# Two layers of decode attention on one core: gate and up by column halves, copies shared by two engines, filler transposes, and another map of the buffer between the layers

## The chip, the core and the metric

The kernel runs on one core of a Trainium2 chip. The metric is the device time of one execution in microseconds (us); the median of several runs counts, and less is better. The core has a matrix engine, TensorE (PE in the profile, with PEld for its weight loads), and three engines for other work: VectorE (DVE), ScalarE (ACT) and GpSimd (POOL). SyncE (SP) issues the large transfers (DMAs) from the chip's memory into the core's buffer, SBUF. TensorE writes its results to PSUM, from which VectorE and ScalarE read.

## The reference

One token for each of two sequences goes through two rounds of attention over a long cache and a gated feed-forward block. Both rounds use the same weights and the same cache. Sizes: 512 features, 32 query heads of 128, 8 key/value heads, 32768 cached positions, 1792 hidden features, all float32.

```python
def _A_ref(x, k_cache, v_cache, wq, wo):          # x: (2, 1, 512)
    q = (x @ wq).reshape(B, 1, 32, 128)            # 32 query heads, 4 to a K/V head
    k, v = repeat(k_cache, 4), repeat(v_cache, 4)  # (2, 8, 32768, 128) each
    p = softmax((q . k) * 128 ** -0.5)
    return (p . v).reshape(B, 1, 4096) @ wo

def _B_ref(x, w_gate, w_up, w_down):
    return (gelu(x @ w_gate) * (x @ w_up)) @ w_down

for _ in range(2):
    x = x + _A_ref(layernorm(x), k_cache, v_cache, wq, wo)
    x = x + _B_ref(layernorm(x), w_gate, w_up, w_down)
```

## The kernel before

**Tiling and buffer.** A (K/V head, sequence) combination is called a pair; a layer has 16 pairs, and layer 1 takes them in the reverse order. All weights, K and V go through one SBUF tile, `mem`, of 104 units. A unit is 512 float32 columns on 128 partitions, 256 KB. K of a pair has 64 units (16 MB), V as well. They come in pieces of 32 units, but for the last two pairs of layer 0 (`K_SPLIT`, `V_SPLIT`), which come in pieces down to 4 units.

**What sets the order of the transfers.** `add` puts every transfer of the program in one list, `stream`, in the order in which it will be needed. `take` finds a place in `mem` for the transfer at the head of the list, `give` returns the place of a piece that has been used, and `pump` issues transfers from the head as long as places are found (L157, the only line that issues loads from SP). For the pieces around the change of layers, `plan` names the place in units: a table written by hand. So a DMA stands in SP's queue until the instructions that read the previous holder of its place are done, and SP issues in order: a DMA that waits holds all DMAs behind it.

**Between the layers.** The last pair of layer 0 is the first of layer 1. Its V (64 units, 0 to 64) and the last `KEEPK` pieces of its K (8 units each) stay in `mem` and aren't loaded again. The remaining units serve, one after the other, `wo` (the output projection's weights), four transfers of gate and up weights (`gu`, 7 units each), four of the down weights (`wd`), four of the query weights of layer 1 (`wq`, 8 units each), and then the remaining K of that pair. The plan of before:

```python
out["gu", 0, i] = [80, 87, 94, 80][i]
out["wd", 0, i] = [88, 92, 96, 100][i]
out["wq", 1, i] = [80, 88, 96, 80][i]
put(K_SPLIT, "k", 1, last, [88, 96, 80, 64, 72, 88])
```

gu 0 and gu 1 have places that are free before the layer's end; gu 2 covers the place of `wo`, and gu 3 that of gu 0.

**A pair.** `scores` (L316) multiplies the queries with the K pieces into the PSUM tile `S`; `softmax` takes the maximum (L320), the exponential (L336) and transposes the probabilities through the PSUM tile `T` (L339, L340); `values` (L358) multiplies them with the V pieces into the PSUM tile `A`; `combine` scales `A` to the SBUF tile `big` (L365, VectorE, 512 columns) and gathers the heads by four products with a selection matrix (L369) into `oT` (L370); after every second pair `project` (L375) multiplies with `wo` into the PSUM tile `W`.

**Between attention and feed-forward.** `residual` copies `W` to SBUF on ScalarE and sums it (L389), and adds the residual and the mean with products on TensorE (L380, L382, L392) into `xin` (L393); `complete`, called later, does the same a second time for the residual stream. `spread` works out the layer norm's scale, with a power on GpSimd (L261). `feedforward` multiplies gate and up by rows of the weights (L419: a transfer holds 128 of the 512 input features, all 1792 columns of both matrices), applies gelu (L428 to L434), transposes (L439, L440) and multiplies with the down weights (L446). `queries` (L283) does the query projection, and scales and transposes the result (L292, L295, L298). `finish` (L406 to L411) writes the output.

## Time and profile before

| | before |
|---|---|
| time, median of 3 runs | 2595.84 us (2595.5 to 2597.18) |
| the profiled execution | 2596.09 us |
| its span | 2594.1 us, so 1.99 us lie around it |
| TensorE busy | 1373.1 us, 53% of the span |
| bytes moved | 1109.86 MB, mean 428 GB/s |
| L316 waiting for K | 549.0 us |
| L358 waiting for V | 497.6 us |

The span runs from the first to the last thing the profiler saw of the kernel. In a row of a timeline stand the start in us, the length, the engine, the line, the operation, what it writes and reads, how many instructions are put together, and in brackets how long the engine was idle before and what ended the wait. In a row of windows stand the stretch, its length, the busy time and number of instructions of PE, PEld, DVE, ACT and POOL, and then three numbers: the granted clock of TensorE as a share of full speed, the busy share of the DMA engines, and GB/s. "SPq" rows are DMAs at the moment of their issue.

### The profile page before, as it was taken

How to read it: one execution, taken by the hardware profiler on the slowest of the kernel's cores; microseconds unless marked ns; L12 is line 12 of the kernel's file. 1: busy time of each engine (PE TensorE's matmuls, PEld its weight loads, DVE VectorE, ACT ScalarE, POOL GpSimd, SP SyncE). 2: the span in 40 equal slices, each digit the busy share in tenths (PEclk: the TensorE clock that was granted, in tenths of full speed). 3: DMA queues.
4: the chain of work that ended last, by engine and by line, in shares of the span. 5: the costliest groups of instructions: out<-in, count | busy, mean ns of one | idle time of the engine just before them, and what ended most of it. 6: DMA issues, size and time to landing. Idle time of an engine off the chain costs nothing.

```text
span 2594.1 us, 20074 instructions
## 1 busy us (share of the span) xinstructions
PE 1373.1 (53%) x9434; PEld 399.3 (15%) x9434; DVE 152.5 (6%) x399; ACT 52.0 (2%) x140; POOL 2.9 (0%) x9
## 2 busy tenths in 40 slices
PE   3654555454445445455577454555555554554556
PEld 1111111111111111111122111111111111111112
DVE  0000000000000000000001000000000000000000
ACT  0000000000000000000000000000000000000000
POOL 0000000000000000000000000000000000000000
PEclk7677767777777777777778777767767767777677
DMA  9999999999999999999999999999999999999997
GB/s 423 431 428 434 432 434 431 432 435 436 429 432 429 435 435 433 429 428 429 409 384 438 433 433 430 433 433 432 433 432 434 432 435 432 430 434 430 436 432 334
DMA packets 28306, 1109.86 MB, mean 428 GB/s; under 512 B 3392, under 2 KB 3520, under 8 KB 3776
## 3 DMA queue, kind: packets, MB, share of 16 engines
q1 hardware_dynamic: 27936, 1108.36, 99.2%
q8 instruction: 74, 1.21, 0.2%
q10 hardware_dynamic: 288, 0.22, 0.0%
q14 instruction: 8, 0.07, 0.0%
HBM read 1108.56 MB, written 0.00 MB: 427 GB/s over the span
## 4 chain that ended last, share of the span: by engine, by line
DMA 59%; PE 27%; another core or an unknown queue 12%; DVE 1%; issue 0%; ACT 0%; SPq 0%; DVEq 0%; ACTq 0%
DMA mem<-in_vt 49%; PE A L358 16%; DMA mem<-in_kt 10%; PE S L316 7%; PE W L375 1%; PE small L369 1%; PE S L419 1%; PE W L446 0%; DVE big L365 0%; PE small L382 0%; DMA mem<-in_wq 0%; PE T L339 0%; DMA mem<-in_gu 0%; PE small L283 0%
## 5 line engine op out<-in xcount | busy, mean ns | idle before, releaser
L316 PE MATMUL S<-mem,qpad 128*32 128x512 f32 x4096 | 590.0, 739 | 550.2 <-DMA mem<-in_kt 549.0
L358 PE MATMUL A<-mem,pT 128*16 128x512 f32 x4096 | 580.8, 729 | 497.7 <-DMA mem<-in_vt 497.6
L316 PEld LDWEIGHTS S<-mem,qpad 128*32 128x32 f32 x4096 | 150.7, 132 | 980.3 <-issue 707.9
L358 PEld LDWEIGHTS A<-mem,pT 128*16 128x16 f32 x4096 | 128.4, 112 | 921.2 <-issue 740.3
L320 DVE TENSOR_REDUCE mx<-S 128x1 f32<-128x512 f32 x64 | 44.3, 692 | 1137.9 <-PE S L316 1137.9
L336 ACT ACTIVATE big<-S,bias 128x512 f32<-128x512 f32 x64 | 43.4, 683 | 2411.5 <-DVE bias L332 2411.5
L339 PE MATMUL T<-cst,big 128*128 128x128 f32 x256 | 54.9, 352 | 68.4 <-ACT big L336 40.4
L365 DVE TENSOR_SCALAR big<-A,linv 128x512 f32<-128x512 f32 x32 | 24.0, 751 | 1056.5 <-PE A L358 1056.5
L369 PE MATMUL small<-cst,big 128*128 128x4 f32 x256 | 36.2, 265 | 29.8 <-DVE big L365 29.8
L340 DVE COPY pT<-T 128x512 f32<-128x512 f32 x64 | 44.3, 692 | 91.6 <-PE T L339 91.6
L339 PEld LDWEIGHTS T<-cst,big 128*128 128x128 f32 x256 | 35.5, 175 | 83.3 <-ACT big L336 67.1
L369 PEld LDWEIGHTS small<-cst,big 128*128 128x128 f32 x256 | 33.4, 204 | 61.4 <-DVE big L365 61.4
L329 PE MATMUL small<-cst,nm 128*128 128x128 f32 x32 | 10.3, 322 | 34.2 <-DVE nm L327 34.2
L283 PE MATMUL small<-mem,xpad 128*32 128x512 f32 x128 | 21.0, 786 | 11.8 <-DMA mem<-in_wq 11.1
L375 PE MATMUL W<-mem,oT 128*2 128x512 f32 x128 | 25.0, 864 | 4.1 <-DVE oT L370 4.1
L419 PE MATMUL S<-mem,xpad 128*32 128x256 f32 x224 | 19.6, 471 | 3.6 <-DMA mem<-in_gu 3.1
L342 PEld LDWEIGHTS small<-ls,cst 128*128 128x128 f32 x64 | 14.4, 276 | 0.0
L329 PEld LDWEIGHTS small<-cst,nm 128*128 128x128 f32 x32 | 4.2, 133 | 64.9 <-DVE nm L327 62.8
L336 ACT ACTIVATION_READ_ACCUMULATOR big<-S,bias 128x1 f32 x64 | 12.6, 196 | 0.0
L446 PE MATMUL W<-mem,pT 128*2 128x512 f32 x56 | 11.3, 913 | 1.0 <-DVE pT L440 1.0
L342 PE MATMUL small<-ls,cst 128*128 128x2 f32 x64 | 11.8, 254 | 0.0
L419 PEld LDWEIGHTS S<-mem,xpad 128*32 128x32 f32 x224 | 9.0, 131 | 11.7 <-issue 4.2
(61 smaller groups left out, 100.2 us busy)
## 6 DMA issues: line engine op xcount, KB each, us to landing
mem<-in_kt SPq DMA_DIRECT2D x24, 2048.0 KB, 38.1
mem<-in_wq SPq DMA_DIRECT2D x8, 2048.0 KB, 10.6
mem<-in_wo SPq DMA_DIRECT2D x16, 1024.0 KB, 51.3
mem<-in_gu SPq DMA_DIRECT2D x8, 1792.0 KB, 39.3
mem<-in_vt SPq DMA_DIRECT2D x3, 4096.0 KB, 43.6
mem<-in_kt SPq DMA_DIRECT2D x2, 6144.0 KB, 37.9
mem<-in_vt SPq DMA_DIRECT2D x3, 2048.0 KB, 48.1
mem<-in_vt SPq DMA_DIRECT2D x6, 1024.0 KB, 51.4
```

The costliest lines, as they stand in the source:

```text
L283: nc.tensor.matmul(qp[32 * t:32 * t + 32, :], window(k, v), w[:, 4 * v + t, :], start=(k == 0 and v == 0), stop=(k == KC - 1 and v == 1))
L316: nc.tensor.matmul(S[32 * t:32 * t + 32, u, :], qpad[:, at_q - 4 * c:at_q + 32 - 4 * c], w[:, QUAD * i + t, :], start=(same_u[0] == 8 * u ...
L320: nc.vector.tensor_reduce(mx[:, u:u + 1], S[:, u, :], axis=AX.X, op=OP.max)
L336: nc.scalar.activation(p[u], S[:, u, :], AF.Exp, bias=bias, scale=SCALE, accum_out=ls[:, u:u + 1])
L339: nc.tensor.transpose(T[:, u, k * P:(k + 1) * P], p[u][:, k * P:(k + 1) * P], ident)
L340: nc.vector.tensor_copy(pT[:, u].rearrange("p k r -> p (k r)"), T[:, u, :])
L342: nc.tensor.matmul(m[:, :2], same, ls, start=True, stop=True)
L358: nc.tensor.matmul(A[32 * t:32 * t + 16, :], pT[:, u, k, 32 * t + 16 * e:32 * t + 16 * e + 16], w[:, QUAD * i + t, :], start=(j == 0), sto ...
L365: nc.vector.tensor_scalar(md, A, linv, None, op0=OP.mult)
L369: nc.tensor.matmul(m[:, :REP], md[:, c * P:(c + 1) * P], head[:, c, :], start=(c == 0), stop=(c == 3))
L375: nc.tensor.matmul(W[32 * t:32 * t + NB, :], oT[:, t, :], w[:, t, :], start=first, stop=final)
L419: nc.tensor.matmul(S[32 * t:32 * t + 32, which, :FN], window(k, v), w[:, FR * which + r, :], start=(k == 0 and v == 0), stop=(k == KC - 1 ...
```

## The change

There are five parts.

1. **The plan.** `KEEPK` is 3, so 24 units of K (64 to 88) stay between the layers, and one K piece of 2 MB fewer is loaded. All other transfers between the layers use the two places 88 to 96 and 96 to 104 in turn, until the kept pieces have been used. The table follows in the diff.
2. **Gate and up by column halves.** The weights are stored anew (`halves`): transfers 0 and 1 hold the first 1024 columns of both matrices (8 units each), 2 and 3 the other 768 (6 units each). The first half accumulates in `S`, the second in `T`, and gelu runs on each half by itself; the down products of the first half come before the transposes of the second.
3. **Shared copies.** `wide` splits a copy of 512 columns from PSUM into a half on ScalarE and a half on VectorE. `combine`, `residual`, `queries` and `finish` use it.
4. **Transposes in place of selection products.** `combine` and `residual` transpose the copy and sum the parts on VectorE; `complete` and its second gather are gone, its addition is one VectorE instruction. The matrix of averages is a broadcast of one column.
5. **Filler transposes.** `warm(n)` puts n transposes of the identity on TensorE, into a PSUM bank that nobody reads then: in the last pair of each layer ahead of every later V piece and in `combine`, further in `residual` and `finish`, after each gate/up transfer, and before the third down transfer.

In the stream, `wo` now stands ahead of a pair's second V piece instead of its last.

```diff
-KEEPK = 2
+KEEPK = 3
...
-    put(K_SPLIT, "k", 0, last, [32, 40, 48, 56, 80, 88, 64, 72])
+    put(K_SPLIT, "k", 0, last, [32, 40, 48, 56, 88, 64, 72, 80])
...
-        out["gu", 0, i] = [80, 87, 94, 80][i]
-        out["wd", 0, i] = [88, 92, 96, 100][i]
-        out["wq", 1, i] = [80, 88, 96, 80][i]
-    put(K_SPLIT, "k", 1, last, [88, 96, 80, 64, 72, 88])
+        out["gu", 0, i] = [88, 96, 88, 96][i]
+        out["wd", 0, i] = [88, 92, 96, 102][i]
+        out["wq", 1, i] = [88, 96, 88, 96][i]
+    put(K_SPLIT, "k", 1, last, [88, 96, 64, 72, 80])
...
+    def wide(dst, src, scale=None, totals=None):
+        h = 256
+        kw = [{}, {}] if totals is None else [{"accum_out": totals[:, i:i + 1]} for i in range(2)]
+        nc.scalar.activation(dst[:, h:], src[:, h:], AF.Copy, scale=1.0 if scale is None else scale, **kw[1])
+        if totals is None:
+            nc.vector.tensor_scalar(dst[:, :h], src[:, :h], 1.0 if scale is None else scale, None, op0=OP.mult)
+        else:
+            nc.vector.tensor_scalar(dst[:, :h], src[:, :h], 1.0, 0.0, op0=OP.mult, op1=OP.add, **kw[0])
+
+    def warm(n, bank=T[:, 0]):
+        for i in range(n):
+            nc.tensor.transpose(bank[:, :P], ident, ident)
...
+        for s, m in parts:
+            if s and n == len(ORDER) - 1:
+                warm(6)
...
-    def combine(linv, oT, b):
+    def combine(linv, oT, b, busy):
         md = big()
-        nc.vector.tensor_scalar(md, A, linv, None, op0=OP.mult)
-
+        wide(md, A, scale=linv)
+        warm(busy)
         m = small()
         for c in range(4):
-            nc.tensor.matmul(m[:, :REP], md[:, c * P:(c + 1) * P], head[:, c, :], start=(c == 0), stop=(c == 3))
-        nc.vector.tensor_copy(oT[:, :, b], m[:, :REP])
+            nc.tensor.transpose(m[:, c * P:(c + 1) * P], md[:, c * P:(c + 1) * P], ident)
+        warm(busy)
+        mt = m[:, :]
+        diag = bass.AP(tensor=mt.tensor, offset=mt.offset, ap=[mt.ap[0], [1, REP], [P + REP, 4], [32, 4]])
+        nc.vector.tensor_reduce(oT[:, :, b], diag, axis=AX.XY, op=OP.add)
...
+    def gathered(totals=None):
+        ws = big()
+        wide(ws, W, totals=totals)
+        warm(3)
+        m = small()
+        for c in range(KC):
+            nc.tensor.transpose(m[:, c * P:(c + 1) * P], ws[:, c * P:(c + 1) * P], ident)
+        ys = wk.tile([P, KC, NB], F32, name="ys")
+        src = m.rearrange("p (c t r) -> p c r t", c=KC, t=4)[:, :, :NB, :]
+        nc.vector.tensor_reduce(ys, src, axis=AX.X, op=OP.add)
+        return ys
...
+        def gelu(e):
+            gt, ut = both[e][:, 0, :FN], both[e][:, 1, :FN]
+            w = big()
+            a, th = w[:, :FN], w[:, FN:]
+            pr = hT[:, 4 + nj * e:4 + nj * e + nj, :].rearrange("p j r -> p (j r)")
+            nc.scalar.activation(a, gt, AF.Square, scale=cube)
+            nc.vector.tensor_scalar(pr, gt, hrr, None, op0=OP.mult)
+            nc.vector.scalar_tensor_tensor(a, a, 1.0, gt, op0=OP.add, op1=OP.mult)
+            nc.scalar.activation(th, a, AF.Tanh, scale=root)
+            nc.vector.tensor_tensor(pr, pr, ut, op=OP.mult)
+            nc.vector.scalar_tensor_tensor(th, th, 1.0, pr, op0=OP.add, op1=OP.mult)
+            return th
...
+            warm(6, A)
+            if i % 2 == 1:
+                th.append(gelu(e))
+        hidden(0, th[0])
+        down(0)
+        hidden(1, th[1])
+        down(1)
+        warm(4, A)
+        down(2)
+        down(3)
```

Where the instructions stand is shown for three places. The names are those of the tiles; "x4" counts equal instructions in a row. First the order in which SP issues the transfers around the change of layers, from the last pair's V on; before:

```order
L157 DMA mem<-in_vt 128x16384
L157 DMA mem<-in_vt 128x8192
L157 DMA mem<-in_vt 128x4096
L157 DMA mem<-in_vt 128x2048
L157 DMA mem<-in_wo 128x2048
L157 DMA mem<-in_vt 128x2048
L157 DMA mem<-in_gu 128x3584 x4
L157 DMA mem<-in_wd 128x2048 x3
L157 DMA mem<-in_wd 128x1024
L157 DMA mem<-in_wq 128x4096 x4
L157 DMA mem<-in_kt 128x4096 x11
```

and in the changed kernel:

```order
L152 DMA mem<-in_vt 128x16384
L152 DMA mem<-in_wo 128x2048
L152 DMA mem<-in_vt 128x8192
L152 DMA mem<-in_vt 128x4096
L152 DMA mem<-in_vt 128x2048 x2
L152 DMA mem<-in_gu 128x4096 x2
L152 DMA mem<-in_gu 128x3072 x2
L152 DMA mem<-in_wd 128x2048 x3
L152 DMA mem<-in_wd 128x1024
L152 DMA mem<-in_wq 128x4096 x4
L152 DMA mem<-in_kt 128x4096 x10
```

`wo` moved ahead of the later V pieces, the gate/up transfers are 8, 8, 6 and 6 units in place of four of 7, and one piece of K is gone.

Second, TensorE from the end of layer 0's last V piece to the first gate/up products; before:

```order
L358 MATMUL A<-mem,pT 16x512 x64
L369 MATMUL small<-cst,big 128x4 x4
L375 MATMUL W<-mem,oT 2x512 x4
L380 MATMUL small<-xpad,cst 128x8
L382 MATMUL small<-cst,big 128x2 x4
L392 MATMUL small<-cst,total 128x8
L419 MATMUL S<-mem,xpad 32x256 x14
L256 MATMUL small<-sq,avg 128x8
L419 MATMUL S<-mem,xpad 32x256 x42
```

and in the changed kernel, where L369 is `values`, L255 a filler, L380 the transposes of `combine`, L390 `project`, L400 to L413 `residual` and L466 gate/up:

```order
L255 MATMUL T<-cst 128x128 x6
L369 MATMUL A<-mem,pT 16x512 x4
L255 MATMUL T<-cst 128x128 x2
L380 MATMUL small<-cst,big 128x128 x4
L255 MATMUL T<-cst 128x128 x2
L390 MATMUL W<-mem,oT 2x512 x4
L255 MATMUL T<-cst 128x128 x3
L400 MATMUL small<-cst,big 128x128 x4
L411 MATMUL small<-xpad,cst 128x8
L413 MATMUL small<-cst,totals 128x8 x2
L255 MATMUL T<-cst 128x128 x2
L466 MATMUL S<-mem,xpad 32x256 x16
```

The selection products (L369 and L382 of before) are transposes, two products take the place of one for the total, and fillers stand between the steps.

Third, VectorE from the last pair's `combine` on, with the engines for which an instruction waits; before (L365 is the copy of 512 columns in `combine`, L393 writes `xin`, L429 to L434 are gelu):

```order
L365 TENSOR_SCALAR big<-A,linv 128x512 [waits DVE_49,PE_49,Activation_49]
L370 COPY oT<-small 128x4 [waits PE_49]
L393 COPY xpad<-small 128x4x2 [waits PE_49]
L254 TENSOR_TENSOR sq<-xpad 128x8 [waits DVE_49]
L258 ISA sq,var<-small,cst 128x8 [waits PE_49]
L258 ISA var 128x1
L263 SCALAR_TENSOR_TENSOR hrr<-rstd 128x1 [waits Pool_49]
L399 COPY xn<-small 128x8 [waits PE_49]
L429 TENSOR_SCALAR big<-big 128x256 [waits Activation_49]
L430 SCALAR_TENSOR_TENSOR big<-S,rstd,big 128x256 [waits DVE_49]
L433 SCALAR_TENSOR_TENSOR big<-big,S 128x256 [waits Activation_49]
L434 SCALAR_TENSOR_TENSOR big<-big,hrr,S 128x256 [waits DVE_49]
```

and in the changed kernel (L248 and L250 are VectorE's halves of a shared copy, L437 to L441 gelu of one half):

```order
L248 TENSOR_SCALAR big<-A,linv 128x256 [waits Activation_49]
L385 TENSOR_REDUCE oT<-small 128x4 [waits PE_49]
L250 TENSOR_SCALAR big,totals<-W 128x256 [waits Activation_49]
L403 TENSOR_REDUCE ys<-small 128x8 [waits PE_49]
L415 TENSOR_TENSOR xpad<-small,ys 128x4x2 [waits DVE_49,PE_49]
L417 TENSOR_TENSOR xn<-ys,xT 128x8
L266 TENSOR_TENSOR sq<-xpad 128x8 [waits DVE_49]
L270 ISA sq,var<-small,cst 128x8 [waits PE_49]
L270 ISA var 128x1
L474 SCALAR_TENSOR_TENSOR hrr<-rstd 128x1 [waits Pool_49]
L475 TENSOR_SCALAR cube<-rstd 128x1
L476 TENSOR_SCALAR root<-rstd 128x1
```

VectorE's half of a copy waits for ScalarE, which holds the other half of the same PSUM tile. Further on in the same order:

```order
L437 TENSOR_SCALAR pT<-S,hrr 128x256 [waits Activation_49]
L438 SCALAR_TENSOR_TENSOR big<-big,S 128x256
L440 TENSOR_TENSOR pT<-pT,S 128x256 [waits DVE_49]
L441 SCALAR_TENSOR_TENSOR big<-big,pT 128x256 [waits DVE_49,Activation_49]
L437 TENSOR_SCALAR pT<-T,hrr 128x256 [waits Activation_49]
L438 SCALAR_TENSOR_TENSOR big<-big,T 128x256
L440 TENSOR_TENSOR pT<-pT,T 128x256 [waits DVE_49]
L441 SCALAR_TENSOR_TENSOR big<-big,pT 128x256 [waits DVE_49,Activation_49]
L448 COPY pT<-small 128x256 [waits PE_49] x2
```

Both halves of gelu stand ahead of the copy L448 of the first half's transposed result, and the first instruction of each, L437, waits for ScalarE, which squares the same PSUM tile.

166 lines of the change are left out of this document (76 added, 90 removed).

## Prediction, on record before the run

> **What bounds the kernel now.** I read the page first: the rate of the transfers over the span, the chain of waits, and the costliest groups.
>
> ```profile
> span 2594.1 us, 20074 instructions
> GB/s 423 431 428 434 432 434 431 432 435 436 429 432 429 435 435 433 429 428 429 409 384 438 433 433 430 433 433 432 433 432 434 432 435 432 430 434 430 436 432 334
> ...
> DMA 59%; PE 27%; another core or an unknown queue 12%; DVE 1%; issue 0%; ACT 0%; SPq 0%; DVEq 0%; ACTq 0%
> ...
> L316 PE MATMUL S<-mem,qpad 128*32 128x512 f32 x4096 | 590.0, 739 | 550.2 <-DMA mem<-in_kt 549.0
> L358 PE MATMUL A<-mem,pT 128*16 128x512 f32 x4096 | 580.8, 729 | 497.7 <-DMA mem<-in_vt 497.6
> ```
>
> The stream runs at some 432 GB/s and falls in two places: slices 19 to 21 (the layer boundary) and the last (the tail). Elsewhere PE waits about 33 us a pair for K and V (1046.6 / 32), so work added to the other 30 pairs, the two-engine copy and four transposes in each `combine`, is covered and costs 0; a pair would have to grow by 30 us to show. The price of a byte, from PE's waits for 2 MB pieces of K:
>
> ```profile
> 1230.16 1.92 PE L316 MATMUL S<-mem,qpad 128*32 128x512 f32 x16 [2.62 <-DMA mem<-in_kt]
> ...
> 1249.70 1.73 PE L316 MATMUL S<-mem,qpad 128*32 128x512 f32 x8 [2.96 <-DMA mem<-in_kt]
> ```
>
> Four pieces in 19.54 us: 4.885 us for 2 MB, 2.443 per MB. Then the timeline of the boundary, from the layer's last V piece to the sixth K piece of layer 1:
>
> ```profile
> 1291.17 1.91 PE L358 MATMUL A<-mem,pT 128*16 128x512 f32 x8 [3.92 <-DMA mem<-in_vt]
> 1293.21 0.75 DVE L365 TENSOR_SCALAR big<-A,linv 128x512 f32<-128x512 f32 x1 [33.82 <-PE A L358]
> 1294.02 1.87 PE L369 MATMUL small<-cst,big 128*128 128x4 f32 x8 [0.93 <-DVE big L365]
> 1296.14 1.89 PE L375 MATMUL W<-mem,oT 128*2 128x512 f32 x8 [0.26 <-DVE oT L370]
> 1298.04 7.26 SPq L157 DMA_DIRECT2D mem<-in_gu  x2
> 1301.48 3.43 PE L419 MATMUL S<-mem,xpad 128*32 128x256 f32 x28 [0.26 <-DVE xpad L393]
> 1305.16 3.65 PE L419 MATMUL S<-mem,xpad 128*32 128x256 f32 x56
> 1311.88 3.36 PE L419 MATMUL S<-mem,xpad 128*32 128x256 f32 x28 [3.06 <-DMA mem<-in_gu]
> 1328.55 3.55 PE L283 MATMUL small<-mem,xpad 128*32 128x512 f32 x16 [0.26 <-DVE xpad L393]
> 1332.35 1.93 PE L283 MATMUL small<-mem,xpad 128*32 128x512 f32 x16
> 1347.66 1.09 PE L295 MATMUL small<-cst,big 128*128 128x128 f32 x4 [1.01 <-DVE big L292]
> ...
> 1372.36 3.22 PE L316 MATMUL S<-mem,qpad 128*32 128x512 f32 x16 [2.88 <-DMA mem<-in_kt]
> ```
>
> From 1291.17 to 1372.36 the queue carried 7 MB of gate/up, 3.5 of down, 8 of queries and 12 of K: 30.5 MB, 74.5 us at the price above, and it took 81.2. So **the boundary now loses 6.7 us**. Unbroken, the last gate/up piece would be there at 1308.3 (7 MB, 17.1 us); it came at 1311.88, 3.6 of the loss, since its DMA stood for a place. That DMA shows what a restart costs:
>
> ```profile
> 1304.97 0.33 SPq L157 DMA_DIRECT2D mem<-in_gu  x1
> ```
>
> Issued at 1304.97, used at 1311.88: 6.91 us for 1.75 MB, which take 4.27. A DMA issued into an empty queue thus lands **2.6 us** late, and one whose place is free less than 2.6 us before its forerunner lands loses the difference. The other 3.1 us of the loss hang on no wait for a place that I can find.
>
> **Bytes.** Three kept pieces in place of two: one 2 MB DMA of K fewer, -4.9 us.
>
> **The boundary in two places of 8 units.** SP issues in order, so a DMA that waits holds all behind it. Each piece needs the piece two ahead of it used up (gate/up also what carried `wo`); before, gu0 and gu1 needed nothing of this layer's end. I count from T, PE's start on the last V piece, taking durations at full clock, and in brackets at half clock, where rows show both. Two more rows for full clock, with the windows that decide which holds:
>
> ```profile
> 1378.22 0.66 PE L339 MATMUL T<-cst,big 128*128 128x128 f32 x4 [1.26 <-ACT big L336]
> 1379.76 1.09 PE L339 MATMUL T<-cst,big 128*128 128x128 f32 x4 [0.88 <-DVE pT L340]
> 1380.99 5.50 PE L358 MATMUL A<-mem,pT 128*16 128x512 f32 x40
> ```
> ```profile
> 1290.93:1304.58 13.65, 11.59 (x64) 6.09 (x64) 1.25 (x4) 0.69 (x2) 0.00 (x0) 0.50 0.63 246
> 1342.10:1345.50 3.40, 3.40 (x18) 1.36 (x10) 0.00 (x0) 0.00 (x0) 0.00 (x0) 0.50 1.05 448
> 1345.50:1348.90 3.40, 2.23 (x10) 1.78 (x9) 0.94 (x4) 0.00 (x0) 0.00 (x0) 0.50 0.97 414
> 1379.68:1383.09 3.41, 3.33 (x18) 1.73 (x22) 0.92 (x3) 0.00 (x0) 0.00 (x0) 0.50 1.01 430
> 1383.09:1386.51 3.42, 3.42 (x36) 0.86 (x32) 0.00 (x0) 0.00 (x0) 0.00 (x0) 1.00 1.00 426
> ```
>
> The third column from the right is the granted clock: 0.50 through the whole chain after V. The window from 1379.68 held 2.1 us of V products at half clock and four transposes, and the next is at full; that from 1342.10 held as much of long products and eight of 128x2, and the next stays at half. So transposes count toward the clock here, and the fillers should; I take them so.
>
> The shared copies do not run side by side: the DVE half waits for the ACT half of the same PSUM tile, and so does the multiply by `hrr` in `gelu` for the square. With half-width rows of the tail (0.47 ACT, 0.48 DVE, below) a copy costs 0.95 and a hand-over, against 0.75 (L365): +0.25, not a gain. [...]
>
> - Project done, so gu1 issued: V 1.05 (1.91), copy 0.95, transposes 0.66 (1.09), reduce 0.16, project 1.05 (1.89), five hand-overs 0.35: T+4.2 (6.35). V pieces now come 2.5 us apart with fillers between, so V is warm and only project is in doubt: 4.7. (Before: 6.9.) gu1 lands at 4.7 + 2.6 + 4.9 = 12.2, not 9.8: **2.4** lost (2.0 to 4.1).
> - `residual` was 1298.04 to 1301.48, 3.44; now copy 0.95 and its sum 0.19, transposes 0.66 (1.09), two total products and an add: 3.7. gu0 starts at 8.4, cold. gu2 takes six of its eight units: 8.4 + three quarters of 3.43 = 11.0, plus 2.6 = 13.6 against 12.2: **1.4** (0 to 1.7).
> - gu3 after three quarters of gu1, which ends PE's spread and fillers at about 12.9: 14.3 + 2.6 = 16.9, before gu2 lands (17.3): 0 (to 1.3). wd0 after two thirds of gu2: 18.7 + 2.6 = 21.3 against 20.9: **0.4** (to 0.9). wd1 to wd3 come behind it; last 29.9.
> - wq0 needs down(0) and down(1). gu3 is used by 22.8; then square 0.47, three DVE operations of 0.48 and the last of 0.48 with hand-overs, 2.5; hidden(0)'s copy, which stands behind them on DVE, 0.45; two products of 1.05 (1.91) with hidden(1) between, 3.4: 29.2 + 2.6 = 31.8: **1.9** (0.4 to 3.8).
> - wq2 needs q0 used, k0 needs q2, wq3 and k1 likewise a piece later: 1.93 (3.55) to use it plus 2.6 is 4.5 (6.15) against the 4.9 in which the piece between them lands, so 0 or 1.3 each. q0 and q2 follow waits and are mostly cold: **1.0** and **1.0**. k2 lies where the first kept piece was: q3, the query copy with its transposes 2.4, and that piece make 6.3 (9.5), plus 2.6 is 8.9 (12.1) against two landings, 9.8 to 11.1: **0.7**. wq3, k1 and gu3 have **0.5** together. From k3 on PE has kept pieces in hand and each place is free early: 0.
>
> Sum 9.3 (3.4 all warm, 15.9 all cold). The 3.1 not placed may recur or lie under these waits; I take 1.7. Boundary 11.0 against 6.7: **+4.3**.
>
> **Edits with one answer.** `wo` ahead of the later V pieces changes no byte ahead of the last one; V's places and the next pairs' are free as early as before. The average as a broadcast, the constants without `sel` and `head`, `complete` as one add on DVE (0.17, beside PE): off the path, 0.
>
> **The tail.** No DMA waits there, before or after: SP issues all of gate/up and down well ahead.
>
> ```profile
> 2555.23 1.05 PE L358 MATMUL A<-mem,pT 128*16 128x512 f32 x8 [0.58 <-DMA mem<-in_vt]
> 2560.19 1.48 PE L358 MATMUL A<-mem,pT 128*16 128x512 f32 x8 [3.91 <-DMA mem<-in_vt]
> 2570.01 3.63 PE L419 MATMUL S<-mem,xpad 128*32 128x256 f32 x28 [0.26 <-DVE xpad L393]
> 2574.11 5.47 PE L419 MATMUL S<-mem,xpad 128*32 128x256 f32 x84
> 2579.70 0.47 ACT L428 ACTIVATE big<-S,rstd 128x256 f32<-128x256 f32 x1 [12.30 <-PE S L419]
> 2581.22 0.48 DVE L430 SCALAR_TENSOR_TENSOR big<-S,rstd,big 128x256 f32<-128x256 f32 x1
> 2584.22 5.30 PE L446 MATMUL W<-mem,pT 128*2 128x512 f32 x28 [0.52 <-DVE pT L440]
> 2589.62 0.60 ACT L406 ACTIVATE big<-W 128x512 f32<-128x512 f32 x1 [7.39 <-PE W L446]
> 2591.56 0.35 SPq L411 DMA_DIRECT2D out<-xn  x1
> ```
>
> From T = 2560.19 to the end 33.9. gu0 starts at 8.4 for 9.8; gate/up then takes 3.4 cold (1.8 warm), the spread and six fillers 1.2, three pieces of 1.8 (3.65 for two above) and twelve fillers 1.4 (by the four transposes of 0.66, whose last 0.2 is its own way through the array, 0.115 each): done at 19.8 (18.2) for 19.4, so the fillers eat what was won. From there to the first down product 3.0 for 4.6; down and four fillers 5.4 for 5.3; finish 2.1 for 2.0; 2.5 after the DMA. 32.8 (31.2 with gu0 warm), so -1.1 or -2.7, and with down and finish cold as well 1.4 above before. I take **-1.6** (-2.7 to +1.4).
>
> **Sum.** -4.9 + 4.3 - 1.6 = -2.2. The profiled run took 2596.09 (1.99 around its span), 0.25 above the median: 2593.9, and by the median 2593.6. Within 0.2% (5.2 us: 2590.65 to 2601.0) is what a measurement here cannot well tell from no change.
>
> **Rivals.**
> 1. Waits stay small: all warm, 3.4 + 1.7 - 6.7 = -1.6, tail -2.7; -4.9 - 1.6 - 2.7 = -9.2, about **2586.6**. For it: fillers in every pause; against: gu0 follows two pauses of copies.
> 2. Slower, by lock-step at half clock: with two places a piece may take 2.3 us to use (4.9 - 2.6); cold it takes 3.4 to 3.6. This decides if project, wq and kept K all run at 0.50, as they did above: 15.9 + 3.1 - 6.7 = +12.3, tail +1.4: +8.8, **2604.6**; half way from my sum to it, 2599. Against: gu and wd before them are long.
> 3. Fillers don't warm: gu1 and gu2 lose 0.9 more, wq0 and the tail 1.0 and 1.4: +3.3 on mine, **2596.9**. [...] The windows quoted speak against it.
>
> **Chances.** My sum 0.50, rival 1 0.18, rival 2 0.12, rival 3 0.20. Mine and the third end within 0.2% save the edges (some 0.03 fast, 0.04 slow): faster 0.21, same 0.63, slower 0.16. Mine alone 2590.5 to 2597; the range takes in most of the first rival and half-cold lock-step: 2588 to 2600.5.
>
> **What the profile will show.** Right: K of the boundary one piece shorter; SP's gu1 at T+4 to 5, PE waiting about 2 us each for gu1, wq0; DVE's half copies starting as ACT's end; 0.50 for one or two windows after V instead of four. Wrong: waits of over 1 us before every wq and K piece (rival 2), no wait but gu1 (rival 1), 0.50 in windows full of fillers (rival 3).

## The result, and the profile after

| | before | after |
|---|---|---|
| time, median of 12 runs each | 2595.65 us (2593.97 to 2599.12) | 2596.81 us (2592.19 to 2600.35) |
| ratio | | 1.0002, interval 0.9994 to 1.001 |
| the profiled execution | 2596.09 us | 2597.87 us |
| its span | 2594.1 us | 2596.0 us |
| bytes moved | 1109.86 MB | 1107.76 MB |
| lost at the layer boundary | 6.7 us | 15.6 us |
| last V piece landed to output landed | 32.83 us | 30.38 us |

No change that the runs can tell from none, as forecast (2593.6 us, 2588.0 to 2600.5). "Lost" is what it was in the prediction: how much later a transfer landed after the one ahead of it than its bytes take at 2.443 us per MB, summed over the boundary. The moments of landing are the completion events of the DMAs in the trace. Between the two profiled executions lie +1.8 us: bytes -4.9, boundary +8.9, tail -2.45, together +1.55; 0.2 are spread over the rest. The forecast was -2.2 in all, so the net came out 3 to 4 us above it, within the 0.2% that is hard to tell from no change; the boundary's share is twice what was forecast for it (+4.3).

The page of the changed kernel (span, rate of the transfers in 40 slices, chain of waits, the two costliest groups):

```profile
span 2596.0 us, 20044 instructions
...
GB/s 423 435 427 432 431 434 434 433 430 435 434 435 431 432 429 435 428 437 423 385 346 434 434 434 434 432 430 435 436 432 430 433 431 435 435 434 429 433 435 350
...
DMA 59%; PE 26%; another core or an unknown queue 13%; DVE 1%; ACT 0%; issue 0%; SPq 0%; ACTq 0%
...
L324 PE MATMUL S<-mem,qpad 128*32 128x512 f32 x4096 | 582.9, 731 | 564.4 <-DMA mem<-in_kt 563.2
L369 PE MATMUL A<-mem,pT 128*16 128x512 f32 x4096 | 582.8, 731 | 490.8 <-DMA mem<-in_vt 490.8
```

The rate dips in the same places as before. At the boundary two slices are now low, 385 and 346 (before: 409 and 384); the last slice has risen from 334 to 350. In the 75 us from the landing of layer 0's last V piece, the windows say the same (columns: stretch, length, busy time and count of PE, PEld, DVE, ACT, POOL, then granted clock, DMA share, GB/s). Before:

```profile
1291.13:1366.13 75.00, 56.60 (x378) 21.95 (x378) 5.54 (x22) 2.26 (x6) 1.10 (x2) 0.73 0.91 374
```

After, the same 75 us and ahead of them four windows of the granted clock:

```profile
1285.78:1306.26 20.48, 15.27 (x153) 7.64 (x149) 2.15 (x13) 0.95 (x3) 0.55 (x1) 1.00 0.69 274
1306.26:1309.68 3.42, 3.42 (x28) 1.77 (x23) 1.27 (x4) 0.98 (x2) 0.00 (x0) 0.50 0.65 212
1309.68:1330.16 20.48, 12.37 (x108) 5.59 (x102) 3.61 (x13) 1.46 (x4) 0.00 (x0) 1.00 0.95 350
1330.16:1340.40 10.24, 7.81 (x34) 1.77 (x34) 0.17 (x2) 0.00 (x0) 0.55 (x1) 0.50 0.86 326
...
1290.84:1365.84 75.00, 50.92 (x384) 19.18 (x384) 7.99 (x34) 3.86 (x10) 1.10 (x2) 0.82 0.87 329
```

The clock is higher than before (0.82 against 0.73) and stays at 1.00 through the whole chain after V, where it was 0.50. PE is busy for less time. And yet 329 GB/s are moved where it was 374: 45 GB/s over 75 us are 3.4 MB, 8 us of transfer. A faster TensorE and a slower boundary: TensorE's speed alone does not explain the loss. The timeline of the boundary, and after the last "..." of the tail (SPq rows are issues of DMAs):

```profile
1291.57 1.05 PE L369 MATMUL A<-mem,pT 128*16 128x512 f32 x8
1292.74 0.47 ACT L246 ACTIVATE big<-A,linv 128x256 f32<-128x256 f32 x1 [38.04 <-PE A L369]
1293.25 0.48 DVE L248 TENSOR_SCALAR big<-A,linv 128x256 f32<-128x256 f32 x1 [35.55 <-ACT big L246]
1293.79 0.66 PE L380 MATMUL small<-cst,big 128*128 128x128 f32 x4 [0.80 <-DVE big L248]
1294.76 1.04 PE L390 MATMUL W<-mem,oT 128*2 128x512 f32 x8
1295.86 4.44 SPq L152 DMA_DIRECT2D mem<-in_gu  x2
1298.41 1.94 PE L466 MATMUL S<-mem,xpad 128*32 128x256 f32 x32
1305.05 2.51 PE L466 MATMUL S<-mem,xpad 128*32 128x256 f32 x32 [3.68 <-DMA mem<-in_gu]
1306.74 0.33 SPq L152 DMA_DIRECT2D mem<-in_gu  x1
1308.96 2.25 PE L466 MATMUL T<-mem,xpad 128*32 128x256 f32 x24
1313.94 1.93 PE L466 MATMUL T<-mem,xpad 128*32 128x256 f32 x24 [1.91 <-DMA mem<-in_gu]
1318.69 1.04 PE L455 MATMUL W<-mem,pT 128*2 128x512 f32 x8 [1.80 <-DVE pT L448]
...
1331.14 3.64 PE L293 MATMUL small<-mem,xpad 128*32 128x512 f32 x16 [1.78 <-DMA mem<-in_wq]
1336.33 3.64 PE L293 MATMUL small<-mem,xpad 128*32 128x512 f32 x16 [1.03 <-DMA mem<-in_wq]
1340.03 0.33 SPq L152 DMA_DIRECT2D mem<-in_wq  x1
1342.53 2.44 PE L293 MATMUL small<-mem,xpad 128*32 128x512 f32 x16 [2.56 <-DMA mem<-in_wq]
1348.82 3.64 PE L293 MATMUL small<-mem,xpad 128*32 128x512 f32 x16 [3.85 <-DMA mem<-in_wq]
...
2564.85 1.05 PE L369 MATMUL A<-mem,pT 128*16 128x512 f32 x8
2571.68 1.94 PE L466 MATMUL S<-mem,xpad 128*32 128x256 f32 x32
2581.73 1.93 PE L466 MATMUL T<-mem,xpad 128*32 128x256 f32 x24 [0.97 <-DMA mem<-in_gu]
2593.47 0.35 SPq L424 DMA_DIRECT2D out<-xn  x1
```

Project (L390) takes 1.04 us and gu0 (L466 at 1298.41) 1.94, both at full clock; the forecast had gu0 cold. The wait of 3.68 us for gu1 and one for wq0 were forecast; those of 1.0 to 3.9 before the other wq were not, and waits of over 1 us before every wq and K piece were named as the sign of rival 2. The sign doesn't tell: in experiment 2, where next to nothing is lost, TensorE waits 1.1 to 3.0 us before every wq too, since a piece takes 4.9 us to come and less to use. The next table goes through the transfers. "Lead" is how long a DMA had been issued when the transfer ahead of it landed. T is the landing of the last V piece, 1290.84.

| transfer | issued at T + | lead | lost | forecast lost |
|---|---|---|---|---|
| gu1 | 5.0 | -0.15 | 4.4 | 2.4 |
| gu2 | 9.1 | 5.0 | 0 | 1.4 |
| gu3 | 15.9 | 1.9 | 1.6 | 0 |
| wd0 | 20.0 | 3.1 | 1.5 | 0.4 |
| wd1, wd2, wd3 | 20.4 to 25.0 | 4.8 to 7.4 | 1.8 | 0 |
| wq0 | 30.6 | 4.3 | 0.4 | 1.9 |
| wq1 | 36.0 | 4.2 | 0.4 | 0 |
| wq2 | 44.0 | 1.5 | 1.3 | 1.0 |
| wq3 | 49.2 | 2.5 | 1.4 | } 0.5 with k1 and gu3 |
| k0 | 54.2 | 3.8 | 1.1 | 1.0 |
| k1 | 61.7 | 2.2 | 1.8 | (above) |
| k2 | 67.4 | 3.1 | 0 | 0.7 |
| sum | | | 15.6 | 9.3, and 1.7 not placed |

By the prediction's rule (a DMA issued less than 2.6 us ahead loses the difference) these leads would lose 2.75 + 0.7 + 1.1 + 0.1 + 0.4 = 5.1 us, which happens to be what rival 1, all warm, had (3.4 + 1.7). Up to the last gate/up piece TensorE was nearly as quick as in rival 1; three of the four query pieces were used at half clock (3.64 us). The other 10.5 of the 15.6 us are losses that the rule does not have.

### The profile page after: what moved, and what is told of

Same layout as the page of the kernel before. It is cut to its first block, busy times and chain, and to the rows that moved or that the text cites. A ratio compares the mean times of both kernels' runs of the same rounds, so it can differ in the third digit from the quotient of the medians.

```text
span 2596.0 us, 20044 instructions
## 1 busy us (share of the span) xinstructions
PE 1350.1 (52%) x9398; PEld 380.2 (15%) x9398; DVE 151.2 (6%) x422; ACT 69.4 (3%) x178; POOL 3.0 (0%) x9
## 2 busy tenths in 40 slices
DMA packets 28163, 1107.76 MB, mean 427 GB/s; under 512 B 3376, under 2 KB 3504, under 8 KB 3760
## 3 DMA queue, kind: packets, MB, share of 16 engines
q8 instruction: 74, 1.21, 0.2%
## 4 chain that ended last, share of the span: by engine, by line
DMA 59%; PE 26%; another core or an unknown queue 13%; DVE 1%; ACT 0%; issue 0%; SPq 0%; ACTq 0%
DMA mem<-in_vt 47%; PE A L369 16%; DMA mem<-in_kt 9%; PE S L324 7%; DMA mem<-in_gu 2%; DMA mem<-in_wq 1%; PE W L390 0%; PE T L347 0%; DMA mem<-in_wd 0%; PE small L380 0%; PE small L293 0%; DVE big L248 0%; ACT big L246 0%; PE W L455 0%
## 5 line engine op out<-in xcount | busy, mean ns | idle before, releaser
L324 PE MATMUL S<-mem,qpad 128*32 128x512 f32 x4096 | 582.9, 731 | 564.4 <-DMA mem<-in_kt 563.2
L369 PE MATMUL A<-mem,pT 128*16 128x512 f32 x4096 | 582.8, 731 | 490.8 <-DMA mem<-in_vt 490.8
L369 PEld LDWEIGHTS A<-mem,pT 128*16 128x16 f32 x4096 | 129.0, 112 | 911.2 <-issue 736.4
L248 DVE TENSOR_SCALAR big<-A,linv 128x256 f32<-128x256 f32 x32 | 15.5, 484 | 1073.2 <-ACT big L246 1073.2
L246 ACT ACTIVATE big<-A,linv 128x256 f32<-128x256 f32 x32 | 15.1, 473 | 1150.6 <-PE A L369 1150.6
L380 PE MATMUL small<-cst,big 128*128 128x128 f32 x128 | 21.5, 291 | 36.5 <-DVE big L248 36.5
L380 PEld LDWEIGHTS small<-cst,big 128*128 128x128 f32 x128 | 13.7, 143 | 64.6 <-DVE big L248 64.6
L390 PE MATMUL W<-mem,oT 128*2 128x512 f32 x128 | 16.6, 592 | 4.6 <-DVE oT L385 4.4
L344 ACT ACTIVATION_READ_ACCUMULATOR big<-S,bias 128x1 f32 x64 | 12.5, 196 | 0.0
L255 PE MATMUL T<-cst 128*128 128x128 f32 x74 | 12.1, 285 | 0.0
```

The costliest lines, as they stand in the source:

```text
L246: nc.scalar.activation(dst[:, h:], src[:, h:], AF.Copy, scale=1.0 if scale is None else scale, **kw[1])
L248: nc.vector.tensor_scalar(dst[:, :h], src[:, :h], 1.0 if scale is None else scale, None, op0=OP.mult)
L324: nc.tensor.matmul(S[32 * t:32 * t + 32, u, :], qpad[:, at_q - 4 * c:at_q + 32 - 4 * c], w[:, QUAD * i + t, :], start=(same_u[0] == 8 * u ...
L344: nc.scalar.activation(p[u], S[:, u, :], AF.Exp, bias=bias, scale=SCALE, accum_out=ls[:, u:u + 1])
L369: nc.tensor.matmul(A[32 * t:32 * t + 16, :], pT[:, u, k, 32 * t + 16 * e:32 * t + 16 * e + 16], w[:, QUAD * i + t, :], start=(j == 0), sto ...
L380: nc.tensor.transpose(m[:, c * P:(c + 1) * P], md[:, c * P:(c + 1) * P], ident)
```

## The experiments

**Theory A:** a DMA needs more lead than 2.6 us to lose nothing, and two places of 8 units don't give it; the clock has little to do with the loss. **Rival B:** the price of 2.6 us holds, and the remaining loss comes from the chain (late steps, cold TensorE). **Rival C:** the fillers don't warm and the boundary is slow for that, the prediction's third rival, whose 2596.9 us is the number that came out.

**1. The price of a place, by itself.** Only pieces of K are streamed, round and round through two, three or four places, with 4 to 16 products per piece; nothing else is computed.

```diff
+    phases = [(2, 8, 4), (2, 8, 8), (2, 8, 16), (3, 8, 8), (3, 4, 4), (4, 4, 4), (2, 8, 12), (3, 8, 16)]
+    for f, (places, units, use) in enumerate(phases):
...
+        for k in range(places):
+            load(k)
+        for k in range(16):
+            for i in range(use):
+                nc.tensor.matmul(S[32 * t:32 * t + 32, f % 2, :], qpad, w[:, i % units, :], start=True, stop=True)
+            if k + places < 16:
+                load(k + places)
```

> Not the reference's computation: only pieces of K stream through the buffer, each used by a few products (the output is a copy of the input). Eight stretches of 16 pieces: 2 places of 2 MB with 4, 8, 16 and 12 products to use a piece, 3 places with 8 and 16, and 3 and 4 places of 1 MB with 4 products. For every DMA the lead (landing of the one ahead minus its own issue) and the time lost (landing minus landing of the one ahead minus 2.443 us per MB) are read. [...] Rival B (the price is 2.6 us less the lead, as in the prediction): nothing lost from 2.6 us of lead on, 1.3 at a lead of 1.3.

Windows of that kernel, one per phase, from the first landing to the last (columns as above). In this order: two places of 8 units with 4, 8 and 16 products; three places with 8; four places of 4 units with 4; three places of 8 with 16. The record of the clock begins at 108.55 us, so the 1.00 of the first row says nothing: there the 4 products took 1.93 us, and at half clock they take 1.91 in the kernel before (the last V piece, at 1291.17).

```profile
8.38:94.51 86.13, 29.02 (x120) 3.04 (x120) 0.17 (x1) 0.00 (x0) 1.00 0.96 370
99.38:187.36 87.98, 48.65 (x240) 8.30 (x240) 0.00 (x0) 0.00 (x0) 0.71 0.92 358
192.25:292.84 100.59, 65.89 (x480) 16.37 (x480) 0.00 (x0) 0.00 (x0) 0.83 0.81 314
297.74:371.38 73.64, 39.68 (x248) 7.53 (x240) 0.00 (x0) 0.00 (x0) 0.81 1.00 427
...
417.99:455.99 38.00, 25.73 (x120) 2.85 (x120) 0.00 (x0) 0.00 (x0) 0.63 1.02 425
...
561.99:635.43 73.44, 56.10 (x480) 14.49 (x480) 0.00 (x0) 0.00 (x0) 0.98 0.98 417
```

From the fourth landing on, a piece of 2 MB takes 5.82, 5.84 and 6.91 us in two places (6.61 with 12 products), where an unbroken stream takes 4.885; in three places 4.91 with 8 products and 4.90 with 16; four places of 1 MB take 2.55 per MB against 2.443, three of them 2.85. With two places even 4 products, 1.9 us of work, cost 0.9 us per piece, though 1.9 + 2.6 is less than the 4.885 in which the other piece lands; with three places 8 and 16 products cost nothing. So what counts here is how early a DMA is issued, and 2.6 us ahead is not enough. Lost per transfer against its lead, in this run and at the layer boundary of the other ten profiles of the kernel, in both without the transfers that a load of instructions fell into (see below):

| lead, us | lost in the stream alone | lost in the other profiles, median |
|---|---|---|
| below 0 | 3.3 to 4.0 | 3.7 and 5.5, the only two |
| 0 to 1.5 | 2.3 (1.7 to 2.8) | 1.8 |
| 1.5 to 2.6 | 0.9 | 1.4 |
| 2.6 to 3.6 | 1.0 (0 to 2.5) | 0.7 |
| 3.6 to 4.6 | 0.1, a quarter over 0.3 | 0.1, a third over 0.3 |
| over 4.6 | 0.0 | 0.0 |

Theory A, but not at every lead. Up to 1.9 us the prediction's rule holds: in all 25 such transfers of the two columns, lead and loss add up to 2.4 to 3.1 us, with a median of 2.8 where the rule has 2.6. (The first row loses more than that because those DMAs were issued 0.5 to 2.7 us after their forerunner had landed.) From 1.9 to 4.6 us the rule has 0.7 at most, and here it fails: 36 of 74 transfers lose over 0.3 us more than it says, up to 2.5. Above 4.6 us, 3 of 190 lose over 0.3. The DMAs that SP issued here after their forerunner had landed took 2.7 to 3.1 us from issue to landing beside their bytes.

Two further things stand in the trace. The program's own instructions are loaded while the data stream: in the changed kernel's trace 74 packets of 16 KB, 1.21 MB, 0.2% of the time of the 16 DMA engines. Transfers that such a load fell into lost up to 1.9 us more at short leads, some of them nothing; above 4.6 us of lead 12 of 46 lost over 0.3 us, up to 1.5 (wd3 of the changed kernel 1.2 at a lead of 7.4). And each transfer of the boundary has 16 completion events in the trace, as many as there are DMA engines, and counts as landed with the last: of gu1 in the changed kernel 14 came by T + 12.5, one at T + 12.8 and the last at T + 14.2, after one such load of 0.89 us at T + 11.6.

So the 10.5 us of the changed kernel that the rule does not have divide in two. 4.8 fall on the four transfers with a load of instructions (gu1 1.7, wd2 and wd3 1.7, k1 1.4 beyond the rule), 5.5 on six without one whose leads lay between 1.9 and 4.3 us (wd0 1.5, wq3 1.3, k0 1.1, gu3 0.9, wq0 and wq1 0.4 each), 0.2 on the rest.

**2. The changed kernel with three places.** The plan alone is undone: 16 units of K kept, so 4.9 us of bytes more, and three places of 8 units.

```diff
-KEEPK = 3
+KEEPK = 2
...
-        out["gu", 0, i] = [88, 96, 88, 96][i]
+        out["gu", 0, i] = [80, 88, 96, 80][i]
-        out["wq", 1, i] = [88, 96, 88, 96][i]
+        out["wq", 1, i] = [80, 88, 96, 80][i]
-    put(K_SPLIT, "k", 1, last, [88, 96, 64, 72, 80])
+    put(K_SPLIT, "k", 1, last, [88, 96, 80, 64, 72, 88])
```

> The changed kernel with 16 units of K kept in place of 24, so that gate/up, down, queries and K use three places of 8 units in turn; 2 MB more are loaded (+4.9 us). Theory A: most leads are above 4.5 us, the boundary loses 2 to 5 us in place of 15.6, and the time falls by 6 to 9 us, to 2588 to 2591. Rival C (what costs is the chain of copies and fillers, not the number of places): the boundary still loses 10 or more, and the time rises, 2597 to 2602.

2588.3 us (2587.6 to 2589.39), ratio 0.997 (0.9959 to 0.9981): faster than both kernels. Its 75 us from the last V piece on:

```profile
1290.73:1365.73 75.00, 50.66 (x410) 18.13 (x410) 8.68 (x35) 3.86 (x10) 1.10 (x2) 0.91 0.98 407
```

The DMA engines are busy for 0.98 of it. All leads are 5.15 us or more, and 0.8 us is lost. So with the same chain and more bytes the loss is gone: rival C falls, for the fillers are the same here and the clock is 0.91. Rival B is not tested by this run, since with these leads its price would cost nothing either; the stream and the table of leads decide against it.

**3. The plan alone, in the kernel before.** The other half of the same question: only the table of places is taken over.

```diff
-KEEPK = 2
+KEEPK = 3
...
-        out["gu", 0, i] = [80, 87, 94, 80][i]
-        out["wd", 0, i] = [88, 92, 96, 100][i]
-        out["wq", 1, i] = [80, 88, 96, 80][i]
-    put(K_SPLIT, "k", 1, last, [88, 96, 80, 64, 72, 88])
+        out["gu", 0, i] = [88, 96, 88, 96][i]
+        out["wd", 0, i] = [88, 92, 96, 102][i]
+        out["wq", 1, i] = [88, 96, 88, 96][i]
+    put(K_SPLIT, "k", 1, last, [88, 96, 64, 72, 80])
```

> The kernel before with the changed plan alone: 24 units of K kept, gate/up (four of 7 units), down, queries and K through the two places 88 and 96. Theory A (two places of 8 leave DMAs less than 5 us of lead): the boundary loses 14 to 20 us in place of 6.7, the tail stays at 32.8, and with 4.9 fewer for the bytes the time rises to 2599 to 2604. Rival C (the loss comes with the copies and fillers of the change): the boundary loses 6 to 9, and the time falls to 2591 to 2594.

2609.74 us (2606.66 to 2612.12), ratio 1.0053 (1.004 to 1.0067). Both the time and the loss are more than expected: in its profiled run 25.8 us are lost, 6.3 on gu1, 5.5 on wq0, 3.65 on k2, and the tail took 34.45 us in place of 32.8.

```profile
1312.09 3.63 PE L419 MATMUL S<-mem,xpad 128*32 128x256 f32 x28 [2.81 <-DMA mem<-in_gu]
1339.40 3.64 PE L283 MATMUL small<-mem,xpad 128*32 128x512 f32 x16 [4.04 <-DMA mem<-in_wq]
```
```profile
1290.79:1365.79 75.00, 51.50 (x286) 21.43 (x290) 5.55 (x22) 2.27 (x6) 1.10 (x2) 0.57 0.77 291
```

Here the half clock of the prediction's second rival did come: project takes 1.89 us, most gate/up and query pieces 3.6 us to use, the clock is 0.57 over the stretch, and 291 GB/s are moved. The kept K, though, ran mostly at full clock (three kept pieces and two more in 10.46 us, at 1.92 each when at full clock). So the change consists of two parts of opposite sign. The plan by itself costs 13.5 us here (2609.74 against 2596.22 in the same runs); in the changed kernel, whose chain is short and warm, it costs 8.5 (2596.8 against 2588.3); and the other edits bring 7 to 8 by themselves (2588.3 against 2596.1).

**4. Without fillers.** `warm` returns at once.

```diff
     def warm(n, bank=T[:, 0]):
-        for i in range(n):
-            nc.tensor.transpose(bank[:, :P], ident, ident)
+        return
```

> The changed kernel without any filler transpose. Theory A (fillers keep the clock up, and what they delay is little): three or more windows at half clock after the last V piece, the last V piece used 0.7 us sooner, project done at T+5 to 6, boundary 15 to 18 us lost, tail 31.5 to 34 us for 30.4; time 2598 to 2601. Rival E (transposes don't count toward the clock): clock as with them, and the time falls by 1 to 2 us, the fillers' own, to 2595.

2597.98 us (2594.72 to 2602.42), 1.2 above the changed kernel, which the spread of either does not let one tell from nothing; 1.0008 of before (0.9999 to 1.0017). The clock does tell:

```profile
1292.78:1303.02 10.24, 8.24 (x54) 4.31 (x54) 1.46 (x8) 0.47 (x2) 0.00 (x0) 0.50 0.59 218
```

0.50 over the chain, where the changed kernel has 1.00, and 0.68 against 0.80 as a mean over the boundary. So the fillers warm, and rival C is out with its mechanism. The boundary loses 17.0 us, 1.4 more than with fillers, and the tail takes 30.40 us, as with them (31.5 to 34 were expected): with two places a faster chain buys little, and the tail's gain over the kernel before does not come from the fillers. One price of the fillers is seen too: the last V piece is used as soon as it is there, at 1290.86, while in the changed kernel it waited 0.73 us (landed at 1290.84, used from 1291.57) behind the fillers of the pieces before.

**5. Transposes by themselves.** TensorE alone, without the attention kernel around it: from rest 160 transposes of 128x128; 48 long products and then 200 transposes; 48 long products and then 120 products of 2 columns.

```diff
+    d = pause()
+    turns(d, 160)
+    d = pause()
+    long(d, 48)
+    turns(d, 200)
+    d = pause()
+    long(d, 48)
+    thin(d, 120)
```

> Not the reference's computation: TensorE alone (the output is a copy of the input). After a pause, 160 transposes; after a pause, 48 products of 512 columns and then 200 transposes; after a pause, the same 48 and then 120 products of 2 columns. If a transpose counts toward the clock by its 128 columns (0.053 us of 1.35 us that a window of 3.4 us needs): at half clock one in 0.18 to 0.21 us makes 0.9 to 1.0 per window, so the first stretch stays at 0.50; at full clock one in 0.115 makes 1.57, so the second stays at 1.00 for all of its 23 us; the third falls to 0.50 within two windows. If transposes don't count: the second falls to 0.50 within two windows as well.

```profile
19.37:22.78 3.41, 2.89 (x14) 2.89 (x15) 3.17 (x9) 0.00 (x0) 1.00 0.01 2
22.78:38.90 16.12, 16.12 (x149) 15.95 (x148) 14.25 (x34) 0.00 (x0) 1.00 0.01 1
49.40:71.30 21.90, 21.90 (x201) 21.75 (x200) 7.45 (x18) 0.00 (x0) 1.00 0.00 1
84.22:100.00 15.78, 15.78 (x76) 15.78 (x76) 5.29 (x14) 0.00 (x0) 0.50 0.01 1
```

The first 14 transposes take 2.89 us, 0.21 each (the record of the clock begins only at 22.78, so the 1.00 of that row says nothing); from there on they take 0.108 each, at a clock of 1.00. So transposes alone lift the clock, in the first stretch too, which was expected to stay at 0.50; 200 of them hold it. Products of 2 columns don't: half from 84.22 on. For the 1.35 us of the expectation the traces of the two kernels show 1.30. The granted clock changes in them at multiples of 3.41 us (261 of 262 stretches between two changes in the kernel before, 255 of 256 in the changed one), and 444 windows of that length at half clock held products of 256 or 512 columns and nothing else: each of the 252 with more than 1.30 us of them (TensorE's busy time, halved) was followed by full clock, each of the 192 with less by half. By that count, 14 transposes lift the clock if each counts with its whole 0.108 us (1.5 us together), and not with 0.053 (0.7), which is an estimate by columns: about a quarter of the 0.215 us of a product of 512 columns, of which two start every 0.43 us at full clock. All transposes here are of float32, 128x128.

**6. Whole copies.** The shared copies are undone, one engine copies 512 columns, and the sum needs one product again.

```diff
-        nc.scalar.activation(dst[:, h:], src[:, h:], AF.Copy, scale=1.0 if scale is None else scale, **kw[1])
-        if totals is None:
-            nc.vector.tensor_scalar(dst[:, :h], src[:, :h], 1.0 if scale is None else scale, None, op0=OP.mult)
+        if totals is None and scale is not None:
+            nc.vector.tensor_scalar(dst, src, scale, None, op0=OP.mult)
+        elif totals is None:
+            nc.scalar.activation(dst, src, AF.Copy)
         else:
-            nc.vector.tensor_scalar(dst[:, :h], src[:, :h], 1.0, 0.0, op0=OP.mult, op1=OP.add, **kw[0])
+            nc.scalar.activation(dst, src, AF.Copy, accum_out=totals)
```

> The changed kernel with every copy whole on one engine, as before: VectorE for the scaled ones, ScalarE with one sum for the residual's (and one product for the total in place of two). If the halves only run one after the other, each copy is 0.2 to 0.3 us shorter here and the residual 0.4: project done 0.2 to 0.3 sooner after the last V product, the tail 0.4 to 0.9 shorter (29.5 to 30.0), the boundary 13 to 16, the time 2594 to 2596.5. If sharing saves time, the tail is 0.5 to 1 longer and the time 2597 to 2599.

```profile
1292.05 0.75 DVE L245 TENSOR_SCALAR big<-A,linv 128x512 f32<-128x512 f32 x1 [34.08 <-PE A L368]
1292.86 0.66 PE L379 MATMUL small<-cst,big 128*128 128x128 f32 x4 [0.57 <-DVE big L245]
1297.00 1.93 PE L464 MATMUL S<-mem,xpad 128*32 128x256 f32 x32
```

The copy takes 0.75 us in place of 0.47 + 0.04 + 0.48 = 0.99 in the changed kernel. gu0 starts 6.2 us after the last V landing, not 7.6. Yet the time is 2595.66 us (2592.87 to 2598.58), 0.9997 of before (0.9988 to 1.0007), which cannot be told from the changed kernel's; 16.4 us are lost at the boundary (13 to 16 were expected), and the tail takes 30.10 us for 30.38. gu1 loses 1.0 us less, but wq0 1.7 and k1 0.9 more, each with a load of instructions. So a chain that is 1.4 us shorter buys nothing that the runs can tell: with two places the loss moves to other transfers.

**7. Lead without giving the bytes back.** 24 units kept, as in the changed kernel, but the room of 16 units is cut into four places of 4, and gate/up, query weights and K come in transfers of half the size. More transfers are under way in the same room.

```diff
-K_SPLIT = {ORDER[-1]: [8] * 8, ORDER[-2]: [8, 8, 8, 8, 8, 24]}
+K_SPLIT = {ORDER[-1]: [4] * 16, ORDER[-2]: [8, 8, 8, 8, 8, 24]}
-KEEPK = 3
+KEEPK = 6
...
+    for i in range(8):
+        out["gu", 0, i] = [88, 92, 96, 100, 88, 92, 96, 100][i]
+        out["wq", 1, i] = [88, 92, 96, 100, 88, 92, 96, 100][i]
```

> The changed kernel with the same 24 units kept and the same 16 units between the layers, but in four places of 4 units: gate/up, query and K pieces there are halved (1 MB or 0.75 MB). Theory A: after the first gate/up pieces the leads are 3.4 to 6.2 us, the boundary loses 5 to 9 us in place of 15.6, and the time falls to 2587 to 2591. Rival D (16 units are too little room in whatever pieces): 12 to 16 us lost, 2594 to 2598.

2587.34 us (2586.31 to 2587.6), ratio 0.9964 (0.9951 to 0.9978). Of the boundary's 15.6 us 5 are left, 1.7 of them on wq0, issued 2.2 us ahead and with a load of instructions. A further kernel aims at that one: it adds the whole copies and puts the transposes and the copy of gelu's first half ahead of the last gate/up pieces, so that down(0) can begin sooner.

```diff
                 th.append(gelu(e))
-        hidden(0, th[0])
+            if i == 2:
+                hidden(0, th[0])
         down(0)
```

> Four places of 4 units with 24 units kept, whole copies, and the transposes of the first gate/up half with their copy ahead of the last gate/up piece, so that the first down product no longer waits for the second gelu. Theory A: the query pieces' first DMA, which lost 1.7 us with four places, gets 5 us of lead and loses nothing; boundary 3 to 5 us, tail 29 to 30, time 2583.5 to 2587. Rival G (after the restarts are gone, the chain from the last V piece to gate/up sets what is left): wq0 loses less but the gate/up pieces as much more, boundary 5 to 7 and time 2587 to 2588.5.

2585.72 us (2585.37 to 2588.12), ratio 0.9964 (0.9951 to 0.9976): the best median of the study, though its runs overlap with those of the kernel before it. wq0 now has a lead of 5.7 us and loses 0.05, as expected; the tail, 30.46 us (30.81 with four places alone), missed the expected 29 to 30. In its profiled run, which was the slowest of the five, other transfers lost instead, a piece of K 1.6 at a lead of 3.5 and wq1 1.1 with a load of instructions: 6.0 in all. Last, the same with 20 units kept and five places of 4:

```diff
-KEEPK = 6
+KEEPK = 5
...
-        out["gu", 0, i] = [88, 92, 96, 100, 88, 92, 96, 100][i]
-        out["wq", 1, i] = [88, 92, 96, 100, 88, 92, 96, 100][i]
+        out["gu", 0, i] = [84, 88, 92, 96, 100, 84, 88, 92][i]
+        out["wq", 1, i] = [92, 96, 100, 84, 88, 92, 96, 100][i]
```

> The kernel of e8_fours_early with 20 units of K kept in place of 24, so that five places of 4 units serve between the layers; 1 MB more is loaded (+2.4 us). Theory A (what is left of the boundary's loss are DMAs with less than 5 us of lead): nearly all leads rise by 2.4 us, the boundary loses 1.5 to 3.5 in place of 6.3, and the time is 2583.5 to 2586, equal or up to 2 below. Rival H (what is left does not hang on the lead, but on instruction fetches and on the chain): 5 to 7 still lost, time 2587 to 2589.

2586.88 us (2586.82 to 2587.11), ratio 0.9964 (0.9951 to 0.9976). All leads are 4.4 us or more and 1.2 us are lost, as theory A had it; the time lies a little above what was expected, next to rival H's. The bytes cost 2.4, the boundary loses 4.8 less, and the tail, 31.78 us, is 1.3 longer. The time is not to be told from the kernel with four places, which moves 1 MB less, but its runs differ by 0.3 us where those differ by 2.8.

**8. Fillers once the restarts are gone.** The kernel with four places and the early half, without fillers (the diff is that of experiment 4).

> The kernel of e8_fours_early without any filler transpose. If the fillers' clock is worth something once the restarts are gone: half clock for some 10 us after V, the first gate/up place free 1.5 to 2.5 us later, boundary 8 to 10 in place of 6.3, tail 30.5 to 32.5, time 2587 to 2590. If the fillers cost as much as they bring, as the comparison with the changed kernel leaves open (2597.98 against 2596.81): 2584.5 to 2586.5.

2589.89 us (2588.16 to 2593.14), ratio 0.9976 (0.9965 to 0.9987), against 2585.72 with fillers. The first 20 us after the last V piece, with fillers:

```profile
1291.30:1311.30 20.00, 16.39 (x162) 8.81 (x165) 3.98 (x16) 1.67 (x4) 0.55 (x1) 0.91 0.84 324
```

and without:

```profile
1291.42:1311.42 20.00, 14.50 (x123) 6.44 (x126) 3.99 (x16) 1.67 (x4) 0.55 (x1) 0.73 0.72 261
```

0.91 of the clock against 0.73. In this kernel the fillers are worth 4 us by the medians (3 by the ratios to before), and no run without them was as fast as the slowest with them; in the changed kernel they are worth 1.2, which can't be told from nothing. Where the time goes is shown only in part. The boundary did not lose the expected 8 to 10 us but 6.7, against 6.0 with fillers, and the tail took 31.89 us for 30.46: 2.1 us, where the two profiled runs lie 2.8 apart.

## Why the prediction was right, and where its terms were not

The likeliest case, no change beyond 0.2%, is what came, at a ratio of 1.0002. The time, 2596.81 us, lies in the range, 3.2 above the forecast, and happens to be that of rival 3, whose mechanism experiments 4, 5 and 8 exclude. That the total stays this near is in part luck: two errors in the boundary's sum have opposite signs, and the tail came out 0.85 us better than forecast.

- **Bytes, -4.9.** Right: one 2 MB piece of K fewer (1107.76 MB against 1109.86).
- **Boundary, +4.3: right in sign, half the size.** It measured +8.9: 15.6 us are lost where 11.0 were counted. The step that failed is the end of "a DMA issued into an empty queue thus lands 2.6 us late, and one whose place is free less than 2.6 us before its forerunner lands loses the difference", namely that nothing is lost from 2.6 us of lead on. It rested on one row, gu3 of the kernel before, whose queue was not even empty: gu2 landed 0.26 us after gu3's issue. As a price for short leads 2.6 is nearly right (2.8). But with 1.9 to 4.6 us of lead up to 2.5 us were lost in the runs, and the loads of instructions were not in the sum. The terms set to 0 or nearly 0 were the ones that went wrong: gu3 (1.6), wd0 (1.5 for 0.4), wd1 to wd3 (1.8) and, with 0.5 for both and gu3, wq3 and k1 (3.2). Of the 3.1 us of the kernel before that hung "on no wait for a place", 2.0 were two transfers with a load of instructions and over 5 us of lead (wq0 and k2), and 0.8 were leads of 4.1 and 4.3 us (wq3 and k3).
- **The clock: too pessimistic in part.** Project and gu0 were warm, so gu2 was issued early enough and lost 0 in place of 1.4. wq0 (0.4 in place of 1.9) and k2 (0 in place of 0.7) came out better for another reason: the transfers ahead of them were late themselves. wd3 landed 4.2 us later than counted while wq0 was issued 0.7 us later, and k2 was issued 9.5 us after wq3's landing, which is the count for half clock. Half clock was there after 1306 for 3.4 us, and over most of the query products. These errors and the one on the price cancel in part.
- **gu1, 2.4: measured 4.4.** It was issued 4.3 us after PE's start on the last V piece (counted: 4.7) and, since that start came 0.7 after the landing, for the fillers' backlog that the prediction did not have, at T + 5.0. With the counted price it would have landed at T + 12.5, and by then 14 of its 16 completions had come; the last one, after the load of instructions, made it T + 14.2.
- **Shared copies run one after the other, +0.25.** Right: 0.99 against 0.75 us. But it had no effect on the time that could be told in this kernel.
- **Tail, -1.6.** Right in sign, measured -2.45 between landings (-2.7 from PE's start, 31.2 against 33.9): gu0 took 1.94 where it was counted cold, the first bound of the range. For a filler the sum has 0.115 us, from four transposes less 0.2 for a way through the array: no run shows that way, and what they show is a transpose every 0.109 us in the changed kernel (L380) and every 0.108 in experiment 5.
- **Fillers warm.** Right, by the windows of the kernel before; experiment 5 shows it in isolation. But they are not what shortened the tail (experiment 4).
- **Rival 2, lock-step at half clock.** Didn't come here as a whole, though most query products ran at half clock; it came in experiment 3, where the chain was the old one, except for the kept K.

Left open: why a transfer with 3 us of lead loses nothing in one case and 2.5 us in another, and how a load of instructions comes to go with a late transfer in one case and not in another. Of the packets of k0 in the changed kernel four that began at T + 56.8 to 57.2 took 1.75 to 2.2 us, where a packet of 16 KB takes 0.61 (the median); what holds them wasn't found. Nor can the runs tell the kernels with four and five places apart.
